# Last keys of two attention tiles: one 128x128 transpose, rounding and subtraction, then four DMAs, with late ends of value products

## The chip, the cores and the metric

The kernel runs on one core of a Trainium2 chip. The metric is device time in microseconds, and a change of more than about 0.2% either way is told apart from no change.

## What is computed

Attention on 8 batches of 8 heads, 576 positions and head width 64, in which only scores within `tau` of the row's maximum survive the softmax, and then a layer with weights `w_in` and `w_out` and the Mish function on all 4608 positions (`x` is the attention's output, positions by 512):

```
scores = scale * np.matmul(q, k.transpose(0, 1, 3, 2))
thresh = np.max(scores, axis=-1, keepdims=True) - tau
scores = np.where(scores >= thresh, scores, -1e9) - max
attn   = np.exp(scores) / (np.sum(np.exp(scores)) + 1e-09)
x      = np.matmul(attn, v)
h      = x @ w_in
out    = (h * np.tanh(softplus(h))) @ w_out
```

All is float32. The kernel gets that precision from TensorE by splitting an operand into a rounded part (`hi`, type fp32r) and the rest (`lo`), and multiplying both.

## The kernel before

Two stages follow each other. In the first, up to about 856 us of the span, attention and the product with `w_in` (`h`) run together; in the second the products with `w_out` run. The change touches the first stage only.

**Tiles.** A pair is two heads; its 2 x 576 query rows are 9 tiles of 128 rows, and there are 32 pairs, so 288 tiles, numbered `g`. The loop over `g` is written out by hand, and TensorE (PE), VectorE (DVE), ScalarE (ACT) and GpSimd (POOL) execute in the written order (class `InOrder`). The DMA queue of SyncE (SP) alone is ordered by a scheduler. In step `g` the loop issues the scores of tile g+1, the transposes of tile g-2, the evacuation of tile g-3, the value products of tile g-5 and some matmuls of `h`.

**A tile's way.** PE forms the scores `s` (two buffers). DVE takes the row maximum, ACT the exponential `e`, DVE masks and sums into `p`, POOL normalises `p`. PE transposes `p` (keys to partitions): four blocks of 128 keys into the PSUM tile `tp` (one buffer) and the last 64 keys, which are left over from 576 = 4 x 128 + 64, into `t5` (shown in the profile as `t`). ACT rounds to `hi`, DVE subtracts to `lo`. Pairs 0 to 3 (`FULL`) are treated in full precision and are not changed.

**The last keys.** For the other pairs, two tiles share one buffer `p`: an even tile `g-1` and the odd tile `g`. On the odd tile the last 64 keys of both are transposed in two transposes of 64 columns each, which land side by side on partitions 0 to 63 of `t5` (`transposes`). `tail_hi` (ACT) rounds these 64 x 256 values into partitions 0 to 63 of the ring `tk`, and `tail_lo` (DVE) writes the rest into partitions 64 to 127, so that one matmul per value product multiplies both. The ring holds 6 tiles of 128 columns.

**Value products.** `values` sums over the keys into a PSUM tile `y`: eight matmuls of the four blocks (`hi` and `lo`) and one or two matmuls on `tk` (`y<-tk`; two where the columns wrap in the ring). There are four products for each pair, after tiles 1, 4, 6 and 8 (`LAST`), 256 or 320 columns wide. `gather` copies the two halves of `y` to `x` and to a helper `yo` and adds them.

**Buffers in PSUM.** `t5`, `y` and `h` come from one pool of three buffers (`tag="ph"`); a new tile must wait until the last reader of the tile before it in that buffer is done: DVE's `tail_lo` for `t5`, ACT's copy to `hst` for `h`, ACT's copies of `gather` for `y`.

**How many `h` matmuls a step gets** stands in tables: `MIX_FIRST` for steps 42 to 77, `MIX` (period 18) for the next 180 steps, `MIX_LAST` for the last 36. Twelve matmuls make one `h` tile.

**SP's queue** carries the loads of `q`, `k` and `v` into the raw buffers (`r`, L316), the copies that join two heads for tile 4 of a pair (`kph`, `kpl`, `qph`, `qpl`, L382 and L384), the store of `h` (`hd<-hst`, L580) and of the last positions of `x` (`xd<-x`, L553). A load of `r` waits until POOL has read the buffer's old content.

Of the kernel before, what the change touches and what calls it, by code (L numbers as in the profile page):

```python
# [15 lines left out]
P = 128  # L16
B, H, S, D = 8, 8, 576, 64
# [5 lines left out]
XSPLIT = (4, 1, 1)  # L23
# [4 lines left out]
FULL = NP  # L28
# [37 lines left out]
    7: [(3, 0, 0, 128)],  # L66
    8: [(3, 128, 0, 128)],
}
MIX = (6, 6, 3, 4, 4, 7, 6, 7, 8, 3, 8, 2, 6, 2, 7, 3, 8, 6)
MIX_FIRST = (6, 6, 3, 4, 4, 7, 3, 7, 11, 3, 8, 2, 6, 2, 7, 5, 8, 6, 4, 6, 2, 5, 4, 7, 6, 7, 8, 3, 8, 2, 6, 2, 7, 3, 8, 6)  # L70
MIX_LAST = (6, 7, 8, 3, 8, 2, 6, 2, 8, 2, 8, 7, 5, 6, 3, 5, 4, 6, 6, 7, 8, 3, 8, 2, 6, 2, 8, 2, 8, 7, 5, 6, 3, 5, 4, 6)
DRAIN = 9
# [1 line left out]
LAST = {1: 0, 4: 1, 6: 2, 8: 3}  # L74
# [3 lines left out]
TK = 6 * P  # L78
# [5 lines left out]
def fv(ap):  # L84
    return ap.bitcast(F32)
# [104 lines left out]
def attention_moe(tc, q, k, v, tau, w_in, w_out, out):  # L190
# [3 lines left out]
    with ExitStack() as outer:  # L194
# [11 lines left out]
        with ExitStack() as first:  # L206
# [21 lines left out]
            with ExitStack() as att:  # L228
# [7 lines left out]
                pst = att.enter_context(tc.tile_pool(name="pst", bufs=1, space=PSUM))  # L236

                tkf, tk, fulls = ptp.tile([P, TK], F32, name="tkf", tag="tk", bufs=1), [], []
                both_e = sm.tile([P, 2, 2, HL + 2 * G], F32, name="e", bufs=1)
                smap, emap, turn = [], [], [0]  # L240
                for i in range(2):
# [133 lines left out]
                def join_heads(g):  # L375

                    made = pairs[g // 9]["ops"]
                    for a in range(2):
                        rows = slice(a * D, (a + 1) * D)
                        col = QCOL[4][a][1] + a * D  # L380
                        for to, k in zip(kpair, (made["k1"], made["k2"])):
                            nc.sync.dma_start(fv(to[rows]), fv(k[a][rows, D:]))  # L382
                        for i, to in enumerate(qpair):
                            nc.sync.dma_start(fv(to[rows, rows]), fv(made["qs"][a][i * D:(i + 1) * D, col:col + D]))  # L384

                def scores(g, t, first, qs, k1, k2, plain, **_):
                    s = smap[g % 2]
                    terms = []
                    if t == 4 and not plain:
                        first = 0  # L390
                        (kh, kl), (qh, ql) = kpair, qpair
                        terms = [(qh, kh), (ql, kh), (qh, kl)]
                    for a, col in () if terms else QCOL[t]:
                        cs = slice(col, col + P)
# [40 lines left out]
                def transposes(g):  # L435

                    both = tiles[g]["both"]
                    odd = g % 2
                    full = g < FULL * 9
                    at = odd * (S + D if full else S)  # L440
                    tp = pst.tile([P, 4, P], F32, name="tp")
                    for c in range(4):
                        nc.tensor.transpose(tp[:, c, :], both[:, at + c * P:at + (c + 1) * P], ident)
                    t5 = None
                    if full:
                        t5 = psh.tile([P, P], F32, name="t5", tag="ph")
                        end = 4 * P + (odd + 1) * D
                        nc.tensor.transpose(t5, both[:, end - P:end], ident)
                    elif odd:
                        t5 = psh.tile([P, 2, P], F32, name="t5", tag="ph")  # L450
                        for i in range(2):
                            nc.tensor.transpose(t5[:D, i], both[:, i * S + 4 * P:(i + 1) * S], ident)
                    return tp, t5

                def evacuate(t, tp, t5, pt):
# [24 lines left out]
                def tails(g):  # L480

                    if g % 2:
                        if not tk:
                            tk.append(ptp.tile([P, TK], F32R, name="tk", bufs=1))
                        at = (g - 1) * P % TK
                        cs = slice(at, at + 2 * P)
                        t5 = tiles[g]["tp"][1][:D].rearrange("p a b -> p (a b)")
                        yield tk[0][:D, cs], tk[0][D:, cs], t5

                def tail_hi(g):  # L490
                    for hi, lo, t5 in tails(g):
                        nc.scalar.copy(hi, t5)

                def tail_lo(g):
                    for hi, lo, t5 in tails(g):
                        nc.vector.tensor_tensor(lo, t5, fv(hi), ALU.subtract)

                def values_full(r, pt, vf, x):
                    main, tail = pt.pop(r)
# [14 lines left out]
                def values(pi, r, pt, vs, x, engine):  # L514
                    hi, lo = pt.pop(r)
                    n = WIDTH[r]
                    a = r // 2
                    y = psh.tile([P, 512], F32, name="y", tag="ph")
                    at = (pi * 9 * P + ROFF[r]) % TK
                    cut = min(n, TK - at)  # L520
                    ends = [(c, m, tk[0][:, (at + c) % TK:][:, :m]) for c, m in ((0, cut), (cut, n - cut)) if m]
                    main = [(0, n, p[:, c, :n]) for c in range(4) for p in (hi, lo)]
                    order = [(4, end) for end in ends]
                    order = [(0, main[0]), *order, *((i // 2, main[i]) for i in range(1, 8))]
                    for i, (c, (off, m, p)) in enumerate(order):
                        nc.tensor.matmul(
                            y[:, off:off + m], vs[:, a, c].rearrange("p a b -> p (a b)"), p,
                            start=i == 0, stop=i == len(order) - 1, skip_group_check=True,
                        )
                    mn = slice(a * D, a * D + D)  # L530
                    ot = slice((1 - a) * D, (1 - a) * D + D)
                    yo = sm.tile([P, 320], F32, name="yo", bufs=1)
                    xs = x[mn, XOFF[r]:XOFF[r] + n]

                    def gather():
                        nc.scalar.copy(xs, y[mn, :n])
                        nc.scalar.copy(yo[mn, :n], y[ot, :n])
                        engine.tensor_tensor(xs, xs, yo[mn, :n], ALU.add)

                    return gather  # L540
# [54 lines left out]
                chores = {}  # L595
                loads = {}
                adds = []
                pieces = []
                ready = []

# [6 lines left out]
                def begin(g):  # L607
                    pi, t = divmod(g, 9)
                    made = pairs[pi]["ops"]
                    tiles[g] = dict(s=scores(g, t, D if g % 2 == 0 or pi >= FULL else 0, **made))  # L610

                def product(g):
                    pi, t = divmod(g, 9)
                    pr = pairs[pi]
                    if t == 1:
                        pr["x"] = sm.tile([P, S], F32, name="x", bufs=2)
                    if t in LAST:
                        if pi < FULL:
                            some, gather = values_full(LAST[t], pr["pt"], pr["ops"]["vf"], pr["x"])
                            pieces.extend((work, None) for work in some[:-1])  # L620
                            pieces.append((some[-1], (gather, pi if t == 8 else None)))
                        else:
                            adds.append(values(pi, LAST[t], pr["pt"], pr["ops"]["vs"], pr["x"], nc.vector if g >= NT - 1 else nc.gpsimd))
# [21 lines left out]
                for g in range(NT + 5):  # L645
# [56 lines left out]
                        if closed is not None:  # L702
                            close_pair(g - XSPLIT[1], closed)
                    if g >= 12 + 9 * FULL and g % 9 == XSPLIT[0]:
                        close_pair(g, (g - XSPLIT[0]) // 9 - 1)
                    for work in chores.pop(g, []):
                        work()
                    for work in reversed(now):
# [40 lines left out]
                        warm_up(WARM[1 + g])  # L749
                    if not ahead and 2 <= g < NT + 2:  # L750
                        tiles[g - 2]["tp"] = transposes(g - 2)
                for step in sorted(chores):
                    for work in chores.pop(step):
                        work()
# [370 lines left out]
```

## Time and profile before

| | |
|---|---|
| median of three runs | 1299.0 us (1298.92 to 1299.88) |
| the profiled execution | 1298.43 us, its span 1296.6 us |
| granted TensorE clock, mean | 0.998 |
| busy: PE, DVE, ACT, POOL | 98%, 87%, 77%, 54% of the span |
| instructions | 27311 |

Busy shares are means over both stages. PE's matmuls overlap in the pipeline, and their ends are modelled, so the durations of single matmuls add up to more than the time that passed; the distance between starts, or the pieces of the chain of work that ended last, give what one costs. All operations of the engines are recorded by a helper on L98, so the profile is read by names of tiles.

### The profile page before, as it was taken

Reading aid. Unit: us, or ns where it says so; the run is one execution under the profiler, and the core shown is the slowest. Engines: PE = TensorE matmul, PEld = TensorE weight load, DVE = VectorE, ACT = ScalarE, POOL = GpSimd, SP = SyncE. Lnnn points to the kernel's source line nnn. Section 1 sums busy time; section 2 is a strip of 40 time slices with the busy share of each in tenths; the row PEclk is TensorE's granted clock in tenths of the full one; section 3 lists DMA queues with packets and bytes.
Section 4 is the critical chain, followed back from the end, with each engine's and each line's share of the span. In section 5 each row is a group of like instructions: output and inputs, shape, how many; then the busy total and the mean of one; then the engine's idle time right before and its main releaser. Section 6 shows DMA issues by size and latency. Waiting matters only on the chain.

```text
span 1296.6 us, 27311 instructions
## 1 busy us (share of the span) xinstructions
PE 1271.5 (98%) x8685; PEld 1154.4 (89%) x8685; DVE 1122.7 (87%) x3006; ACT 1000.0 (77%) x2060; POOL 695.8 (54%) x871
## 2 busy tenths in 40 slices
PE   8889999999999999999999999999999999999998
PEld 7667889988898898898998899878799999999998
DVE  7888999999999999999999999969868777878774
ACT  6889888888888888888888888776666676667663
POOL 5898877778778777787787777634000000000000
PEclk9999999999999999999999999999999999999999
DMA  6434544444444444454444444267544434443340
GB/s 218 148 112 114 147 121 137 129 121 147 130 124 144 118 141 129 117 148 133 124 135 124 144 128 117 76 204 244 187 146 131 155 131 147 164 153 110 119 125 33
DMA packets 151487, 177.43 MB, mean 137 GB/s; under 512 B 30000, under 2 KB 117040, under 8 KB 151344
## 3 DMA queue, kind: packets, MB, share of 16 engines
q1 hardware_dynamic: 148896, 171.37, 43.9%
q10 hardware_dynamic: 2448, 4.33, 0.9%
q8 instruction: 69, 1.13, 0.4%
q14 instruction: 74, 0.61, 0.1%
HBM read 109.05 MB, written 48.23 MB: 121 GB/s over the span
## 4 chain that ended last, share of the span: by engine, by line
PE 87%; DVE 6%; POOL 2%; ACT 2%; DMA 2%; issue 1%; SPq 0%; DVEq 0%; ACTq 0%; POOLq 0%
PE h L98 25%; PE y L98 19%; PE s L98 12%; PE x L98 10%; PE tp L98 9%; PE z L98 8%; PE t L98 2%; PE hx L98 2%; DVE un L98 2%; DVE p L98 1%; DVE st L98 1%; DVE dec L98 1%; DMA hd<-hst 1%; ACT e L98 0%; POOL dec L98 0%
## 5 line engine op out<-in xcount | busy, mean ns | idle before, releaser
L98 POOL TENSOR_SCALAR p<-p,st 128x576 f32<-128x576 f32 x288 | 240.5, 835 | 106.2 <-DVE st L98 95.9
L98 DVE SCALAR_TENSOR_TENSOR p<-s,st,e 128x580 f32<-128x580 f32 x288 | 236.4, 821 | 16.7 <-ACT e L98 6.0
L98 ACT ACTIVATE e<-s,st 128x580 f32<-128x580 f32 x288 | 215.6, 749 | 31.8 <-DVE st L98 23.9
L98 DVE TENSOR_REDUCE st<-s 128x1 f32<-128x580 f32 x288 | 218.2, 757 | 0.5
L98 PE MATMUL h<-xh,w1h 128*128 128x512 f32 x528 | 215.3, 408 | 0.0
L98 PE MATMUL h<-xl,w1h 128*128 128x512 f32 x528 | 211.9, 401 | 1.0 <-DVE xl L98 1.0
L98 PE MATMUL s<-k,q 128*128 128x290 f32 (+1 forms) x1056 | 195.6, 309 | 15.4 <-DVE p L98 15.2
L98 PE MATMUL h<-xh,w1l 128*128 128x512 f32 x528 | 209.7, 397 | 0.0
L98 PEld LDWEIGHTS s<-k,q 128*128 128x128 f32 x1056 | 168.9, 189 | 45.6 <-DVE p L98 26.5
L98 ACT CAST hi<-tp 128x512 fp32r<-128x512 f32 (+1 forms) x280 | 150.1, 547 | 74.8 <-PE tp L98 69.4
L98 DVE TENSOR_TENSOR ring<-un,ring 128x512 fp32r<-128x512 f32 x252 | 157.3, 690 | 54.4 <-ACT ring L98 54.3
L98 DVE TENSOR_TENSOR lo<-tp,hi 128x512 fp32r<-128x512 f32 (+1 forms) x280 | 173.7, 629 | 25.6 <-ACT hi L98 23.9
L98 PEld LDWEIGHTS tp<-ident,p 128*128 128x128 f32 x1152 | 142.0, 140 | 42.1 <-issue 4.7
L98 PE MATMUL tp<-ident,p 128*128 128x128 f32 x1152 | 173.3, 273 | 3.0 <-ACT pf L98 1.1
L98 ACT CAST ring<-un 128x512 fp32r<-128x512 f32 x252 | 138.9, 619 | 33.7 <-DVE un L98 33.0
L98 PE MATMUL y<-hi,vs 128*128 128x256 f32 (+1 forms) x448 | 135.3, 317 | 0.0
L98 PE MATMUL x<-ring,un 128*128 128x256 f32 x1152 | 134.7, 276 | 0.0
L98 PEld LDWEIGHTS x<-ring,un 128*128 128x128 f32 x1152 | 132.6, 188 | 0.0
L98 PE MATMUL y<-lo,vs 128*128 128x256 f32 (+1 forms) x448 | 123.1, 297 | 0.0
L98 POOL TENSOR_TENSOR x<-x,yo 64x256 f32<-64x256 f32 (+1 forms) x111 | 89.2, 804 | 55.4 <-ACT yo L98 54.4
L98 DVE TENSOR_TENSOR un<-un 128x1024 f32<-128x1024 f32 (+1 forms) x94 | 111.0, 1235 | 8.1 <-ACT un L98 8.1
L98 PEld LDWEIGHTS h<-xh,w1l 128*128 128x128 f32 x528 | 99.4, 188 | 13.4
(104 smaller groups left out, 2559.9 us busy)
## 6 DMA issues: line engine op xcount, KB each, us to landing
un<-hd SPq DMA_DIRECT2D x74, 512.0 KB, 4.7
hd<-hst SPq DMA_DIRECT2D x128, 256.0 KB, 2.6
r<-q SPq DMA_DIRECT2D x120, 160.0 KB, 2.8
r<-k SPq DMA_DIRECT2D x120, 160.0 KB, 2.3
r<-v SPq DMA_DIRECT2D x56, 160.0 KB, 2.4
kph<-k SPq DMA_DIRECT2D x56, 144.0 KB, 2.6
kpl<-k SPq DMA_DIRECT2D x56, 144.0 KB, 2.8
dec<-w_in SPq DMA_DIRECT2D x24, 256.0 KB, 2.9
```

Source lines behind the costliest of these rows:

```text
L98: made = method(*args, **kwargs)
```

## The change

1. The last keys of the odd tile are now read from the left end of its scores: `k` holds the last 64 keys ahead of all keys, and odd tiles of all pairs use keys in the order last 64, then 0 to 511 (`begin`, `join_heads`). With this the last keys of the even and of the odd tile lie next to each other in `p`, and one transpose of 128 columns brings them to `t5`: the even tile on partitions 0 to 63, the odd tile on 64 to 127.
2. ACT rounds 128x128 values into a new buffer `swap[:, 0]`, DVE subtracts into `swap[:, 1]`. Engines keep the partition here, and the ring needs `hi` on partitions 0 to 63 and `lo` on 64 to 127, so four DMAs of 64x128 values (32 KB each) on SP's queue carry `swap` into `tk`.
3. In `values` the matmuls on `tk` move from the second place to just before the last. A product of an even tile runs its first seven matmuls at the beginning of its step; the rest follows at the step's end, behind the step's transposes, and its `gather` in the next step. `close_pair` comes one step later for pairs whose last tile is even.
4. `yo` has no buffer of its own any more; it lies in the end of `r12`, which is unused then.
5. `MIX` is another distribution of the same 96 matmuls of `h` over 18 steps. `MIX_FIRST` and `MIX_LAST` stay.

```diff
-MIX = (6, 6, 3, 4, 4, 7, 6, 7, 8, 3, 8, 2, 6, 2, 7, 3, 8, 6)
+MIX = (6, 8, 2, 4, 2, 8, 6, 7, 10, 3, 8, 2, 4, 4, 5, 3, 8, 6)
...
+                swap = ptp.tile([P, 2, P], F32R, name="swap", bufs=1)
...
-                            nc.sync.dma_start(fv(to[rows]), fv(k[a][rows, D:]))
+                            nc.sync.dma_start(fv(to[rows]), fv(k[a][rows, first:first + S]))
...
-                        t5 = psh.tile([P, 2, P], F32, name="t5", tag="ph")
-                        for i in range(2):
-                            nc.tensor.transpose(t5[:D, i], both[:, i * S + 4 * P:(i + 1) * S], ident)
+                        t5 = psh.tile([P, P], F32, name="t5", tag="ph")
+                        nc.tensor.transpose(t5, both[:, 4 * P:5 * P], ident)
...
+                def tail_hi(g):
                     if g % 2:
+                        nc.scalar.copy(swap[:, 0], tiles[g]["tp"][1])
+
+                def tail_lo(g):
+                    if g % 2:
+                        nc.vector.tensor_tensor(swap[:, 1], tiles[g]["tp"][1], fv(swap[:, 0]), ALU.subtract)
                         if not tk:
                             tk.append(ptp.tile([P, TK], F32R, name="tk", bufs=1))
...
+                        for i in range(2):
+                            at = (g - 1 + i) * P % TK
+                            for j in range(2):
+                                to = tk[0][j * D:(j + 1) * D, at:at + P]
+                                nc.sync.dma_start(fv(to), fv(swap[i * D:(i + 1) * D, j]))
...
-                    order = [(0, main[0]), *order, *((i // 2, main[i]) for i in range(1, 8))]
...
+                    order = [*((i // 2, main[i]) for i in range(7)), *order, (3, main[7])]
+                    def run(n0, n1):
+                        for i, (c, (off, m, p)) in enumerate(order):
+                            if n0 <= i < n1:
...
-                    yo = sm.tile([P, 320], F32, name="yo", bufs=1)
+                    yo = r12.rearrange("p a b -> p (a b)")[:, -320:]
...
+                            if g % 2:
+                                run(0, 10)
+                                adds.append(gather)
+                            else:
+                                run(0, 7)
+                                finish.append((run, gather))
...
-                        close_pair(g, (g - XSPLIT[0]) // 9 - 1)
+                        pi = (g - XSPLIT[0]) // 9 - 1
+                        close_pair(g + (pi + 1) % 2, pi)
...
+                    while finish:
+                        run, gather = finish.pop(0)
+                        run(7, 10)
+                        adds.append(gather)
```

Three places show what that does to the order. The first is PE around the transposes of tile 157 and the product of the even tile 154, in the middle of the stage. Before (`t_7099` is the two transposes; the product of tile 154 had already ended):

```order
L98 MATMUL h<-xh,w1l 128x512
L98 MATMUL h<-xh,w1h 128x512
L98 MATMUL tp<-ident,p 128x128 x4
L98 MATMUL t_7099<-ident,p 64x128 x2
L98 MATMUL h<-xl,w1h 128x512
```

After, the same place:

```order
L98 MATMUL h<-xh,w1l 128x512
L98 MATMUL h<-xh,w1h 128x512
L98 MATMUL tp<-ident,p 128x128 x4
L98 MATMUL t_7219<-ident,p 128x128
L98 MATMUL y<-tk,vs 128x256
L98 MATMUL y<-lo,vs 128x256
L98 MATMUL h<-xl,w1h 128x512
```

One transpose stands where two stood, and behind it come the last two matmuls of the product of tile 154.

The second place is PE at tile 45, in the stretch of `MIX_FIRST`, with the numbers of the tiles. Before, behind the two transposes of `t5_2088`, the tile `h_2031` ends and the next one, `h_2121`, begins:

```order
L98 MATMUL tp_2083<-ident_76,p_1924 128x128 x4
L98 MATMUL t5_2088<-ident_76,p_1924 64x128 x2
L98 MATMUL h_2031<-xl_1755,w1h_92 128x512
L98 MATMUL h_2031<-xh_1754,w1l_93 128x512
L98 MATMUL h_2121<-xh_758,w1h_92 128x512
```

After, three matmuls of the product `y_2060` stand between (it wraps in the ring, so it has two on `tk`):

```order
L98 MATMUL tp_2087<-ident_76,p_1933 128x128 x4
L98 MATMUL t5_2092<-ident_76,p_1933 128x128
L98 MATMUL y_2060<-tk_1752,vs_1390 128x192
L98 MATMUL y_2060<-tk_1752,vs_1390 128x128
L98 MATMUL y_2060<-lo_1865,vs_1390 128x320
L98 MATMUL h_2042<-xl_1759,w1h_92 128x512
L98 MATMUL h_2042<-xh_1758,w1l_93 128x512
L98 MATMUL h_2134<-xh_759,w1h_92 128x512
```

In the built program `h_2121` lay in the buffer of an older `y`; `h_2134` lies in the buffer of `t5_2092`, which was written a few rows ahead, and its first matmul waits for a DVE instruction.

The third place is SP's queue in the middle of the stage. Before:

```order
L382 DMA kph<-k_3497 64x576
L382 DMA kpl<-k_3498 64x576
L580 DMA hd_68<-hst 128x512
L316 DMA r<-q 128x320 x2
L316 DMA r<-k 128x320 x2
L580 DMA hd_68<-hst 128x512
```

After:

```order
L494 DMA tk<-swap 64x128 x4
L384 DMA kph<-k_3541 64x576
L581 DMA hd_68<-hst 128x512
L384 DMA kpl<-k_3542 64x576
L317 DMA r<-q 128x320
L494 DMA tk<-swap 64x128 x2
L317 DMA r<-q 128x320
L494 DMA tk<-swap 64x128 x2
L317 DMA r<-k 128x320 x2
L581 DMA hd_68<-hst 128x512
```

The four copies to the ring stand between the loads; the first two of a group carry the rounded part and wait for ACT, the next two wait for DVE. Here the second two stand behind a load of `q`.

More of the change, by code (lines that the diff above doesn't have):

```diff
@@ L377, in join_heads @@
                     made = pairs[g // 9]["ops"]
+                    first = D if (g + 4) % 2 == 0 else 0
                     for a in range(2):
@@ L439, in transposes @@
                     full = g < FULL * 9
-                    at = odd * (S + D if full else S)
+                    at = odd * (S + D)
                     tp = pst.tile([P, 4, P], F32, name="tp")
@@ L478, in lo_main @@
                         nc.vector.tensor_tensor(lo[:, :, dst], tp[:, :, src:src + n], fv(hi[:, :, dst]), ALU.subtract)
-                def tails(g):
+                def tail_hi(g):
                     if g % 2:
+                        nc.scalar.copy(swap[:, 0], tiles[g]["tp"][1])
+                def tail_lo(g):
+                    if g % 2:
+                        nc.vector.tensor_tensor(swap[:, 1], tiles[g]["tp"][1], fv(swap[:, 0]), ALU.subtract)
                         if not tk:
                             tk.append(ptp.tile([P, TK], F32R, name="tk", bufs=1))
[L485 to L496, printed above, removed]
+                        for i in range(2):
[3 more added lines that the diff above has]
+                                nc.sync.dma_start(fv(to), fv(swap[i * D:(i + 1) * D, j]))
                 def values_full(r, pt, vf, x):
@@ L523, in values @@
                     order = [(4, end) for end in ends]
-                    order = [(0, main[0]), *order, *((i // 2, main[i]) for i in range(1, 8))]
[L525 to L529, printed above, removed]
+                    order = [*((i // 2, main[i]) for i in range(7)), *order, (3, main[7])]
+                    def run(n0, n1):
+                        for i, (c, (off, m, p)) in enumerate(order):
+                            if n0 <= i < n1:
+                                nc.tensor.matmul(
+                                    y[:, off:off + m], vs[:, a, c].rearrange("p a b -> p (a b)"), p,
+                                    start=i == 0, stop=i == len(order) - 1, skip_group_check=True,
+                                )
                     mn = slice(a * D, a * D + D)
                     ot = slice((1 - a) * D, (1 - a) * D + D)
-                    yo = sm.tile([P, 320], F32, name="yo", bufs=1)
+                    yo = r12.rearrange("p a b -> p (a b)")[:, -320:]
                     xs = x[mn, XOFF[r]:XOFF[r] + n]
@@ L538, in gather @@
                         engine.tensor_tensor(xs, xs, yo[mn, :n], ALU.add)
-                    return gather
+                    return run, gather
                 def operands_x():
@@ L597, in attention_moe @@
                 adds = []
+                finish = []
                 pieces = []
@@ L609, in begin @@
                     made = pairs[pi]["ops"]
-                    tiles[g] = dict(s=scores(g, t, D if g % 2 == 0 or pi >= FULL else 0, **made))
+                    tiles[g] = dict(s=scores(g, t, D if g % 2 == 0 else 0, **made))
                 def product(g):
@@ L622, in product @@
                         else:
-                            adds.append(values(pi, LAST[t], pr["pt"], pr["ops"]["vs"], pr["x"], nc.vector if g >= NT - 1 else nc.gpsimd))
+                            engine = nc.vector if g >= NT - 1 else nc.gpsimd
+                            run, gather = values(pi, LAST[t], pr["pt"], pr["ops"]["vs"], pr["x"], engine)
+                            if g % 2:
[4 more added lines that the diff above has]
+                                finish.append((run, gather))
                 def close_pair(g, pi):
```

## The prediction

> **What bounds the kernel.** I read the stretches of the span first, then the chain of work that ended last, then the groups. In the stretches the columns after the length are busy us (and instructions) of PE, PE's weight loads, DVE, ACT and POOL, then the granted clock and the DMA engines' share:
>
> ```profile
> 130.00:140.00 10.00, 7.57 (x40) 6.55 (x41) 9.85 (x28) 7.13 (x19) 9.59 (x13) 0.83 0.52 146
> 140.00:150.00 10.00, 9.94 (x60) 8.56 (x59) 9.50 (x30) 8.14 (x18) 7.92 (x10) 1.00 0.49 143
> 400.00:500.00 100.00, 100.00 (x650) 90.05 (x649) 95.16 (x298) 84.85 (x182) 78.33 (x96) 1.00 0.44 128
> 820.00:840.00 20.00, 20.00 (x134) 18.19 (x133) 19.08 (x60) 14.42 (x29) 9.66 (x12) 1.00 0.13 45
> PE s L98 <- DVE p L98: 15.2, 22, 1.2
> ```
>
> From about 140 to 856 us PE has no gap, and DVE is 95% busy behind it. The last row is PE's largest wait in all: 15.2 us in 22 waits. The chain says whether a "busy" PE really sets the pace. Its shares from 141 to 856 us, and then its pieces around tiles 154 to 156 (start, length, matmuls):
>
> ```profile
> by line: PE h L98 43.2%; PE s L98 19.1%; PE y L98 18.7%; PE tp L98 15.1%; PE t L98 3.8%; POOL x L98 0.1%; issue 0.0%; POOLq L98 0.0%
> 470.71 0.44 PE tp L98 x4
> 471.15 0.22 PE t L98 x2
> 471.37 0.70 PE h L98 x3
> 472.07 0.53 PE s L98 x4
> 472.60 0.93 PE h L98 x4
> 473.53 0.44 PE tp L98 x4
> 473.97 1.06 PE y L98 x9
> ...
> 378.39 1.40 PE y L98 x10
> ```
>
> The chain runs through PE alone, matmul after matmul. So in this stage a matmul less is time less, and every new wait of PE is time more. One transpose costs 0.11 us, a matmul of `h` 0.23, a 256-wide one of `y` 0.12, the four of `s` 0.53. The last row is a 320-wide product with two parts on the ring, together as wide as one: 1.40 / 9 = 0.156 for each 320 columns. The `t` transposes are 3.8% of 715 us = 27 us; half of them go.
>
> **The change part by part.** The rows of the last keys, with those that bound their new shapes:
>
> ```profile
> L98 PE MATMUL t<-ident,p 128*64 128x128 f32 x252 | 48.4, 274 | 0.0
> L98 DVE TENSOR_TENSOR tk<-t,tk 64x256 fp32r<-64x256 f32 x126 | 52.7, 418 | 3.9
> L98 DVE TENSOR_TENSOR lo<-tp,hi 128x512 fp32r<-128x512 f32 x224 | 152.8, 682 | 17.9 <-ACT hi L98 16.2
> L98 DVE TENSOR_TENSOR lo<-tp,hi 128x256 fp32r<-128x256 f32 x56 | 20.9, 416 | 7.7 <-ACT hi L98 7.7
> L98 ACT COPY hst<-h 128x512 f32<-128x512 f32 x132 | 77.5, 587 | 27.2 <-PE h L98 21.3 <-DMA hd<-hst 2.7 <-ACT dec L98 1.6
> ```
>
> (1) The transpose. 252 become 126. The chain belongs to PE from tile 41 on, so 124 odd tiles count: 124 x 0.11 = 13.6 us off the path. The new one has 128 weight columns instead of 64; its price I take as that of a `tp` transpose, 0.44 / 4 = 0.11, the same. The Trainium skill, "TensorE: Matmul & The Clock Gate", section "Back-to-back issue gap", gives about 81 ns as the sustained distance of matmuls with 128 columns. By that the gain would be an estimated 10.0 us and the sum below 1294.8; the chain's 0.11 us is float32 in this kernel, and the measurement decides.
>
> (2) DVE's subtraction. 64x256 takes 418 ns and 128x256 takes 416, so partitions do not count and columns do: 266 ns for 256 columns. 128x128 is then 416 - 133 = 283 ns, 0.135 us less. ACT's rounding shrinks alike. Neither is on the path; both only bring the data earlier. I count nothing.
>
> (3) The four DMAs, and when they must land. These rows show tile 155, DVE over one pair of tiles, and tile 45:
>
> ```profile
> 470.98 0.38 PE L98 MATMUL t<-ident,p 128*64 128x128 f32 x2
> 471.67 0.36 ACT L98 CAST tk<-t 64x256 fp32r<-64x256 f32 x1
> 472.70 0.42 DVE L98 TENSOR_TENSOR tk<-t,tk 64x256 fp32r<-64x256 f32 x1
> ...
> 467.63 0.82 DVE L98 SCALAR_TENSOR_TENSOR p<-s,st,e 128x580 f32<-128x580 f32 x1
> 473.15 0.82 DVE L98 SCALAR_TENSOR_TENSOR p<-s,st,e 128x580 f32<-128x580 f32 x1
> ...
> 153.76 0.38 PE L98 MATMUL t<-ident,p 128*64 128x128 f32 x2
> 155.32 0.42 DVE L98 TENSOR_TENSOR tk<-t,tk 64x256 fp32r<-64x256 f32 x1
> ```
>
> And the transfers (KB, median us to landing), the issue time of one of 64 partitions, and SP's longest kind of wait:
>
> ```profile
> un<-hd SPq DMA_DIRECT2D x74, 512.0 KB, 4.7
> hd<-hst SPq DMA_DIRECT2D x128, 256.0 KB, 2.6
> r<-q SPq DMA_DIRECT2D x120, 160.0 KB, 2.8
> r<-k SPq DMA_DIRECT2D x120, 160.0 KB, 2.3
> kph<-k SPq DMA_DIRECT2D x56, 144.0 KB, 2.6
> xd<-x SPq DMA_DIRECT2D x32, 32.0 KB, 2.2
> L382 SPq DMA_DIRECT2D kph<-k x56: 461/467/468, 107.3 to 816.9; - x56
> DMA to landing us min/median/max: 2.3/2.6/5.3
> SPq L316 <- POOL q L98: 205.2, 111, 4.5
> ```
>
> No row shows a copy from SBUF to the ring. Its landing lies between the 2.2 us of `xd<-x` (32 KB, the same size) and the 5.3 of the slowest `kph<-k`; I take 2.2, the nearest in size, and 0.47 us for the issue of each. For tile 155 ACT ends at 472.03, so the two rounded parts are issued by 473.0; DVE ends at 473.12 - 0.14 = 472.98, the even tile's rest is issued at about 473.1 and lands at 475.3. The even product of tile 154 is the tightest I find. In the new order 2 + 7 matmuls of `y`, 8 of `h`, 8 of `s` and 9 transposes stand between the start of that tile's transpose and `y<-tk`: 1.06 + 1.86 + 1.06 + 0.99 = 5.0 us, at 476.0. That leaves 0.7 us. An odd product (all four needed, its `y<-tk` eighth) has about 5.9 us after its transpose: landing at 475.8 is 4.8, margin 1.1. So I put the usual wait at zero and 0.5 us in all for stragglers; were all at 5.3 us, see the rivals. The old place of `y<-tk`, second in the product, had no such room. SP itself gets 504 issues of 0.47 us, 1.9 us for every 5.7 us of two tiles, in a queue that already waits (last row); a group can stand behind a load that waits for POOL, as the third quoted place of the order shows, up to 4.5 us. Loads of `r` come later too, by up to 1.9 us; ACT, 85% busy, takes that.
>
> (4) The late ends keep `y`'s buffer a step longer, and there are three buffers. Where `MIX_FIRST` and `MIX_LAST` rule, the second quoted place of the order comes twice in each: tiles 45, 63, 261, 279. The new `h` needs the buffer of a `t5` transposed just before. From the rows of tile 45: transpose at 153.76, DVE done at 155.74, 1.98 us, minus 0.14 = 1.84. PE arrives after one transpose (0.11), `y` of 192, 128 and 320 columns (0.31) and two `h` (0.47): 0.89. PE waits 0.95 us, four times 3.8 us. In `MIX` no `h` begins that close: counted in the same way, the narrowest places in its order leave 1.8 us for a `t5`, just what it takes here, and 1.1 us for a copy of `h` of 0.59 (last row of the fence above); zero. Bounds: nothing (if an earlier wait absorbs it) and, with tile 155's 2.14 us instead of 1.98, 4 x 1.1.
>
> (5) DVE's pace. From mask to mask two tiles take DVE 473.15 - 467.63 = 5.52 us without a gap; after, 5.38. PE's work from the transpose of tile 155 to that of 157 falls to 5.0, and `tp` has one buffer: PE must wait for DVE's subtraction there. Over 18 tiles DVE needs 9 x 5.38 = 48.4 us, PE about 50.9, so it is local: I take 0.15 us per 18 tiles, 14 such stretches, 2.1 us; bounds 0 and the whole 0.38, 5.3 us.
>
> (6) `yo` in `r12`, the other order of keys, `close_pair` and the new `MIX` have the same instructions as before; POOL's sums move by one step, and POOL is 78% busy there. Nothing, with the later closing covered because the last pair of a batch is odd and not delayed.
>
> **Sum.** -13.6 + 3.8 + 2.1 + 0.5 = -7.2 us. The profiled execution took 1298.43 us (0.6 below the median of the runs); 1298.4 - 7.2 = 1291.2 us. With the waits at their lower bounds it is 1284.8.
>
> **Rivals.**
> (A) The gain comes whole, 1284.8 us: the waits fall where PE would have waited anyway, or DVE's earlier end covers them. For it: PE waits nowhere today. Against it: the wait at tile 45 follows from two rows.
> (B) DVE becomes the pace-maker. The four tiles 153 to 157 hold the transposes closest; at the whole 0.38 us in (5) the sum is -13.6 + 3.8 + 5.3 + 0.5 = -4.0, 1294.4; with a second such place per 18 tiles it is 1298 and nothing is left. For it: DVE's 95%. Against it: DVE loses 0.135 us per two tiles where PE loses 0.11.
> (C) The ring is late, and the kernel is slower. A wait per even product begins when the rest lands 0.7 us later than I put it, at 2.9 us. With the four even products in 18 tiles 0.3 to 0.4 us apart in room (about 5.0, 5.4, 5.8 and 6.2 us after the transpose), landing at 4.0 us costs 1.1 + 0.7 + 0.3 = 2.1 us per 18 tiles, 14 times 29 us: 1320. It outweighs the gain of 7.2 from about 3.35 us on (0.5 us per 18 tiles). For it: twice the issues on SP, and its wait of up to 4.5 us for POOL. Against it: medians of 2.3 to 2.8 us for four to five times the bytes.
> (D) The four copies land one after the other, each 2.2 us after the last: the third lands at 472.1 + 6.6 = 478.7, 2.7 us late, and over four products 8.4 us per 18 tiles: about 1410. The rows speak against it: 74 x 4.7 + 128 x 2.6 + 120 x 2.8 + 120 x 2.3 + 56 x 2.6 = 1439 us of flights in a span of 1296.6, so flights overlap. The Trainium skill, "DMA: Bandwidth & Descriptors", section "Rules for kernel authors", says that two transfers to disjoint halves of the partitions serialize and that one of 128 partitions should be used; that is this rival, if it held for latency and not only for bandwidth.
>
> **Chances.** My forecast (some of the gain eaten in PSUM and on DVE, 1287 to 1295.5) 0.56, A 0.16, B 0.12, C 0.14, D 0.02. Within 0.2% is 1296.4 to 1301.6, about what a measurement tells from no change. Faster: 0.56 + 0.16 + half of B = 0.78, and I take 0.76, since waits may add up; same 0.10; slower 0.14. The range reaches from A, 1284.5, to the edge of B and the beginning of C, 1299.5.
>
> **What would show it.** Right: `t` with 126 matmuls, the `tk` subtraction at about 283 ns, PE still without gaps from 400 to 500 us, four waits of PE's `h` for DVE near 0.9 us at tiles 45, 63, 261 and 279. Wrong: PE waiting for DMA at `y<-tk` (C), for DVE's `lo` at `tp` more than 0.2 us per 18 tiles (B), or ACT waiting for `r`. The prediction fails if SP's queue falls behind, which no row of before can show.

## The result, and the profile after

The changed kernel takes 1316.1 us (median of four runs, 1315.8 to 1317.0), beside 1299.1 for the kernel before on the same chip: ratio 1.0131, interval 1.0113 to 1.0148. It is slower by 17 us, where 1291.2 was forecast and 1299.5 was the upper end. The profiled span is 1315.2 us.

The stretch from 400 to 500 us, in which PE had no gap before (columns as in the prediction):

```profile
400.00:500.00 100.00, 97.24 (x609) 85.33 (x609) 87.16 (x287) 79.21 (x178) 77.63 (x95) 1.00 0.53 154
```

PE, DVE and ACT are idler, DVE most (95.16 before). So PE no longer sets the pace alone, and DVE does not set it either. The shares of the chain that ended last, by line, name a new member:

```profile
PE h L98 24%; PE y L98 16%; PE x L98 10%; PE s L98 10%; PE z L98 7%; PE tp L98 7%; PE hx L98 4%; DMA tk<-swap 4%; DVE st L98 2%; ACT e L98 2%; DVE p L98 1%; PE t L98 1%; ACT hi L98 1%; POOL k L98 1%; SPq L494 1%
```

The copies to the ring are 4% of 1315 us, and SP's issue of them (L494) 1%. The waits (who, for whom: us in total, times, longest; PEld is PE's weight loads) say where this reaches PE:

```profile
PE y L98 <- DMA tk<-swap: 15.9, 23, 1.5
PEld h L98 <- DVE swap L98: 6.9, 11, 1.1
PE h L98 <- DVE swap L98: 2.6, 4, 0.7
```

PE's matmuls stand idle for the ring 15.9 us in `y<-tk`, and 2.6 us with `h` for the buffer of a `t5`. (The 6.9 us of the loads contain these four waits once more and are not added.) Shorter gaps count too: below, a delay is the distance between the starts of two neighbouring matmuls less the usual distance of such a pair, summed over 141 to 870 us. In this measure `y<-tk` is delayed by 23.0 us. The operations themselves have the sizes of the forecast; these are the groups from 141 to 870 us, with tile shapes:

```profile
L98 DVE TENSOR_TENSOR swap<-t,swap 128x128 fp32r<-128x128 f32 x123 | 34.6, 281 | 1.1 <-DMA tk<-swap 1.1
L98 ACT CAST swap<-t 128x128 fp32r<-128x128 f32 x123 | 33.7, 274 | 2.8 <-DMA tk<-swap 2.6
L98 PE MATMUL t<-ident,p 128*128 128x128 f32 x123 | 33.7, 274 | 0.0
```

The flights are no longer than forecast either (issue time and landing of line L494):

```profile
L494 SPq DMA_DIRECT2D tk<-swap x504: 461/552/1751, 129.5 to 873.8; - x168
...
DMA to landing us min/median/max: 1.7/1.9/4.5
```

A copy lands 1.9 us after the start of its issue, sooner than the 2.2 us assumed. What is late is the issue. Here is SP's queue up to 491 us (start, length):

```profile
485.03 0.38 SPq L554 DMA_DIRECT2D xd<-x  x1
485.53 0.37 SPq L317 DMA_DIRECT2D r<-q  x1
485.94 0.47 SPq L386 DMA_DIRECT2D qpl<-q  x1
486.46 0.59 SPq L386 DMA_DIRECT2D qph<-q  x1
487.39 0.46 SPq L386 DMA_DIRECT2D qpl<-q  x1
487.96 3.14 SPq L494 DMA_DIRECT2D tk<-swap  x4
491.20 0.55 SPq L384 DMA_DIRECT2D kph<-k  x1
```

DVE's subtraction for the four copies, and PE's product that reads them:

```profile
486.17 0.28 DVE L98 TENSOR_TENSOR swap<-t,swap 128x128 fp32r<-128x128 f32 x1
```

```profile
491.69 0.22 PE L98 MATMUL y<-tk,vs 128*128 128x128 f32 x1
492.54 0.33 PE L98 MATMUL y<-tk,vs 128*128 128x192 f32 x1 [0.63 <-DMA tk<-swap]
```

DVE has both parts ready at 486.45. SP comes to the copies at 487.96 and needs 3.14 us for four, back to back; the issue of the last begins at 490.52, and it lands 1.89 us later, at 492.4. PE stands at the ninth matmul of the product (the second on the ring) for 0.63 us. The chain of waits has the same piece:

```profile
489.92 0.55 SPq L494
490.52 1.89 DMA tk<-swap
492.54 0.49 PE y L98 x2
```

For comparison, SP's queue before, at about the same place in the program:

```profile
471.24 0.47 SPq L382 DMA_DIRECT2D kph<-k  x1
472.49 0.33 SPq L553 DMA_DIRECT2D xd<-x  x1
472.86 0.47 SPq L382 DMA_DIRECT2D kpl<-k  x1
473.38 0.59 SPq L384 DMA_DIRECT2D qph<-q  x1
474.27 1.31 SPq L316 DMA_DIRECT2D r<-q  x1
```

It had gaps. Over 300 to 800 us SP issued 441 DMAs before, 38% of the time; after it is 769 of 0.53 us each, 82%, and the median gap between two is 0.09 us. That is 82 issues for 18 tiles, 82 x 0.62 = 51 us, as much as PE's own work in 18 tiles (50.9 in the prediction). The queue has next to no slack left. The issue of the even tile's rest (third copy) begins 2.0 us after DVE's end (median of the groups of tiles 79 to 257), not 0.1, and it lands 4.0 us after DVE's end.

### The profile page after: what moved, and what is told of

It is laid out like the page before. It is cut to its first block, busy times and chain, and to the rows that moved or that the text cites. A ratio compares the mean times of both kernels' runs of the same rounds, so it can differ in the third digit from the quotient of the medians.

```text
span 1315.2 us, 28340 instructions
## 1 busy us (share of the span) xinstructions
PE 1270.1 (97%) x8559; PEld 1141.6 (87%) x8559; DVE 1091.3 (83%) x3006; ACT 981.6 (75%) x2060; POOL 694.4 (53%) x871
## 4 chain that ended last, share of the span: by engine, by line
PE 79%; DVE 5%; ACT 4%; DMA 4%; issue 3%; POOL 3%; SPq 1%; DVEq 0%; POOLq 0%; ACTq 0%
PE h L98 24%; PE y L98 16%; PE x L98 10%; PE s L98 10%; PE z L98 7%; PE tp L98 7%; PE hx L98 4%; DMA tk<-swap 4%; DVE st L98 2%; ACT e L98 2%; DVE p L98 1%; PE t L98 1%; ACT hi L98 1%; POOL k L98 1%; SPq L494 1%
## 5 line engine op out<-in xcount | busy, mean ns | idle before, releaser
L98 DVE TENSOR_REDUCE st<-s 128x1 f32<-128x580 f32 x288 | 218.1, 757 | 13.6 <-PE s L98 12.9
L98 PE MATMUL y<-hi,vs 128*128 128x256 f32 (+1 forms) x448 | 130.9, 315 | 0.0
L98 POOL TENSOR_TENSOR x<-x,un 64x256 f32<-64x256 f32 (+1 forms) x111 | 89.5, 806 | 76.4 <-ACT un L98 68.7
L98 PE MATMUL y<-lo,vs 128*128 128x256 f32 (+1 forms) x448 | 126.0, 297 | 0.0
L98 PEld LDWEIGHTS h<-xh,w1h 128*128 128x128 f32 x528 | 99.7, 189 | 16.6 <-DVE swap L98 6.9
```

The lines of the kernel that those rows point to most:

```text
L98: made = method(*args, **kwargs)
```

## The experiments

| kernel | us, median | ratio to before, interval |
|---|---|---|
| the change | 1316.1 | 1.0131 (1.0113 to 1.0148) |
| `reorder`: order alone | 1309.7 | 1.0074 (1.0059 to 1.0089) |
| `reorder_old_mix`: order alone, old `MIX` | 1315.6 | 1.0126 (1.0109 to 1.0143) |
| `no_copies`: the change without the four DMAs | 1296.5 | 0.9973 (0.9961 to 0.9984) |
| `two_copies`: two of the four | 1310.8 | 1.0079 (1.0064 to 1.0094) |
| `idle_copies`: before and four unread DMAs | 1303.4 | 1.0031 (1.0021 to 1.0040) |
| `light_sp`: the change, 16 of SP's 82 issues less | 1298.9 | 0.9999 (0.9990 to 1.0008) |
| `mix_all`: the change, `MIX` everywhere | 1314.7 | 1.0118 (1.0104 to 1.0132) |
| `light_mix`: both | 1296.8 | 0.9983 (0.9974 to 0.9992) |
| `direct_old`: one transpose, no `swap`, old order | 1300.5 | 1.0010 (1.0000 to 1.0019) |
| `direct_late`: the same in the new order | 1316.2 | 1.0130 (1.0115 to 1.0145) |
| `h_on_act`: the change, stores of `h` on ACT's queue | 1334.8 | 1.0272 (1.0252 to 1.0292) |
| `pool_moves`: POOL in the place of the DMAs | 1329.0 | 1.0229 (1.0215 to 1.0243) |

**`reorder`.** The kernel before with the late ends, the new `MIX` and `yo` in `r12`; two transposes and direct writes into the ring stay.

```diff
-                    order = [(0, main[0]), *order, *((i // 2, main[i]) for i in range(1, 8))]
+                    order = [*((i // 2, main[i]) for i in range(7)), *order, (3, main[7])]
...
+                                run(0, 7)
+                                finish.append((run, gather))
```

> The kernel before with the changed order alone (late ends of value products, the new MIX, yo in r12); two transposes and direct writes to the ring as before, no copies on SP. Theory 1, SP's queue is full (in the changed kernel 769 issues between 300 and 800 us, 0.53 us each, are 82% of the time, and about 0.1 us of waiting on the queue's own semaphores goes with each: 99%): the order costs only the PSUM buffer at four places, about 4 us, so 1299 to 1304. Theory 2, the copies are late by their own latency, not by the queue: the same, 1299 to 1304. Theory 3, the new order of PE itself loses the time (buffers of PSUM, single tp buffer): 1312 or more, and PE waits as long as in the changed kernel, but not for DMA.

The order alone costs 10.6 us, between the two ranges of the expectation. The lag behind the kernel before (difference of the starts of the same tile's transposes in the two traces) jumps by 1.2 to 1.3 us at tiles 45, 63, 261 and 279, and grows by 0.63 us for every 18 tiles between, under `MIX`, from 3.2 us at tile 78 to 9.5 at tile 258. PE at tile 45 shows the jump (in brackets the idle time before, and for whom):

```profile
153.55 0.38 PE L98 MATMUL t<-ident,p 128*64 128x128 f32 x2
...
154.37 0.40 PE L98 MATMUL h<-xh,w1l 128*128 128x512 f32 x1
155.70 0.47 PE L98 MATMUL h<-xh,w1h 128*128 128x512 f32 x1 [0.93 <-DVE tk L98]
```

The new `h` starts 1.33 us after the matmul ahead of it instead of 0.23. The growth between comes from the same wait: the trace has it at one tile of each 18 (number 83, 101, 119 and so on), about 0.5 us each time.

`reorder` has the long subtraction of before (418 ns). In the changed kernel the same place at tile 45 reads, on PE and on DVE:

```profile
154.51 0.27 PE L98 MATMUL t<-ident,p 128*128 128x128 f32 x1
...
155.23 0.40 PE L98 MATMUL h<-xh,w1l 128*128 128x512 f32 x1
156.27 0.50 PE L98 MATMUL h<-xh,w1h 128*128 128x512 f32 x1 [0.65 <-DVE swap L98]
...
155.94 0.28 DVE L98 TENSOR_TENSOR swap<-t,swap 128x128 fp32r<-128x128 f32 x1
```

The `h` stands idle for 0.65 us there and starts 1.04 us after the matmul ahead of it, a delay of 0.81.

**`reorder_old_mix`.** The same with the table of before.

```diff
-MIX = (6, 8, 2, 4, 2, 8, 6, 7, 10, 3, 8, 2, 4, 4, 5, 3, 8, 6)
+MIX = (6, 6, 3, 4, 4, 7, 6, 7, 8, 3, 8, 2, 6, 2, 7, 3, 8, 6)
```

> The kernel before with late ends, but with its old MIX: only that table differs from the run with the order alone. Theory, the order's loss is the new h that must wait for the buffer of a t5 written just ahead: in the traces that place costs 1.3 us at tiles 45, 63, 261 and 279, where the old tables rule, and 0.7 us per 18 tiles where the new MIX rules. With the old MIX it is there once in all 18 tiles: 14 x 1.3 = 18 us, 1315 to 1320. Rival, the late ends themselves cost (a y held a step longer, later sums): the table makes no difference, 1308 to 1312.

1315.6 us. In the groups the kind of matmul with which an `h` tile begins waits 13.1 us for DVE's `tk`, nearly twice the 7.2 of the same group in `reorder`:

```profile
L98 PE MATMUL h<-xh,w1h 128*128 128x512 f32 x528 | 214.0, 405 | 13.1 <-DVE tk L98 13.1
```

The lag grows by 1.23 us for 18 tiles under `MIX` instead of 0.63. Nothing else differs, so the growth is where `h` tiles begin, next to a `t5` that has just been written. The new table halves it and does not end it.

**`no_copies`.** The change without the four DMAs; the ring holds zeros, so the part of the last 64 keys is missing from the result.

```diff
+                            nc.vector.memset(fv(tk[0]), 0.0)
...
-                                nc.sync.dma_start(fv(to), fv(swap[i * D:(i + 1) * D, j]))
```

> The changed kernel without the four copies: the ring is set to zero once, so the last 64 keys of the rows from pair 4 on are missing in the output; the engines' work is the same. Theory 1 and 2: with the copies gone the gain of the transpose appears, -13.6 us and some +4 to +6 of waits for PSUM and DVE: 1289 to 1294. Theory 3: the loss stays, over 1305.

1296.5 us, above the 1289 to 1294 expected: 13.3 less than `reorder` (one transpose, smaller operations and the other order of keys), 19.7 less than the change (the copies). PE is nearly without gaps from 400 to 500 us:

```profile
400.00:500.00 100.00, 99.81 (x636) 88.18 (x635) 90.84 (x302) 82.13 (x184) 78.41 (x97) 1.00 0.45 131
```

From the kernel before over `reorder` and `no_copies` to the change these are three steps, 10.6 - 13.3 + 19.7 = 17.0 us. Such steps add up whatever the kernels do; that each would cost the same without the others is not shown by it, and `direct_late` below speaks against it.

**`two_copies`.** Only the rest (`lo`) is copied; its rounded part is missing from the result.

```diff
-                            for j in range(2):
+                            for j in (1,):
```

> The changed kernel with only the two copies of the unrounded rest (those that wait for DVE, the later ones); the rounded part of the last 64 keys from pair 4 on is missing in the output. SP issues 64 instead of 82 per 18 tiles. Theory 1: 64 x 0.64 = 41 us of 51, the queue keeps up, few waits at y<-tk, 1290 to 1296. Theory 2: the critical copy is still there, with the same latency behind DVE, so the waits at y<-tk stay: 1308 or more.

1310.8 us: half the copies take 14.3 of the 19.7 us, although SP's share of issue time from 300 to 800 us is only 59%. Of 13.8 us of delay at `y<-tk`, 11.9 stand at one product of each 18 tiles, that of tile 154 and of every 18th tile beside it, which the prediction found the tightest. For tile 190 SP, DVE and PE show why:

```profile
581.40 1.74 SPq L384 DMA_DIRECT2D kph<-k  x1
583.23 0.55 SPq L384 DMA_DIRECT2D kpl<-k  x1
583.83 0.59 SPq L386 DMA_DIRECT2D qph<-q  x1
584.47 0.59 SPq L386 DMA_DIRECT2D qpl<-q  x1
585.11 0.59 SPq L386 DMA_DIRECT2D qph<-q  x1
585.80 1.19 SPq L495 DMA_DIRECT2D tk<-swap  x2
...
582.08 0.28 DVE L98 TENSOR_TENSOR swap<-t,swap 128x128 fp32r<-128x128 f32 x1
...
587.79 0.35 PE L98 MATMUL y<-tk,vs 128*128 128x256 f32 x1 [1.72 <-DMA tk<-swap]
```

The data are ready at 582.36, and the copies stand behind five joins (the copies that join two heads) until 585.80. The first join is here one of the long issues (1.74 us); at tiles where it is not, the delay of this product is mostly about 0.7 us. So the cost is not in proportion to the number of copies, and it does not need a full queue: what stands directly ahead of the copies counts. In the change the same product has 11.4 of the 23.0 us; the other half is spread over other products, where `two_copies` has 1.9.

**`idle_copies`.** The kernel before, and four DMAs for each odd tile from the ring to a place that nobody reads.

```diff
+                        idle = r12.rearrange("p a b -> p (a b)")[:, -TK:]
...
+                                nc.sync.dma_start(idle[part, at:at + P], fv(tk[0][part, at:at + P]))
```

> The kernel before, with four copies of the same size per odd tile out of the ring into unused space; nothing reads them. Theory 1: SP needs 82 x 0.64 = 52.5 us per 18 tiles against 52.0 of PE, so the loads of q, k, v and the stores of h run late and the kernel gets slower though nobody waits for the copies: 1302 to 1320. Theory 2: nobody waits for them, 1299 to 1300.

1303.4 us. SP issues as much as in the change (85% of 300 to 800 us), and that costs 4.3 us. So a full queue is cheap here where no product waits for the copies.

**`light_sp`.** The joins are made for the first changed pair only, so tile 4 of the later pairs multiplies old values and its result is wrong. This takes load from SP and leaves the copies as they are.

```diff
-                    if g % 9 == 0 and FULL <= g // 9 < NPAIRS:
+                    if g == 9 * FULL:
                         join_heads(g)
```

> The changed kernel with the copies that join two heads for tile 4 (kph, kpl, qph, qpl) made for the first of the changed pairs only; tile 4 of the later pairs multiplies these old values. That takes 16 of about 82 issues per 18 tiles from SP's queue and nothing from any engine. Theory (the ring is late because SP issues without a pause): SP's share falls from about 99% to about 82%, the even tile's rest is issued about 1 us after DVE's end instead of 2.0, PE's waits for the ring fall from 23 us to 6 to 14, and the time is 1300 to 1309 us. Rival 1 (not the load but the place of the copies behind a burst of stores and loads): the waits stay near 14 to 20 us, 1309 to 1314. Rival 2 (the flight of the copies itself is too long for the place): 1315 to 1317, as the changed kernel.

1298.9 us, 17.2 less than the change, with all four copies in place and the same order on PE. SP's share is 63%. The median flight is 1.9 us as in the change; the issue of the even tile's rest now begins 0.5 us after DVE's end instead of 2.0. PE's waits for the ring:

```profile
PE y L98 <- DMA tk<-swap: 2.2, 4, 0.9
```

2.2 us instead of 15.9; the delay at `y<-tk` is 5.2 us instead of 23.0, and the difference, 17.8, is about the gain. SP's queue has gaps again:

```profile
470.01 0.33 SPq L317 DMA_DIRECT2D r<-k  x1
470.96 0.33 SPq L317 DMA_DIRECT2D r<-v  x1
471.80 0.33 SPq L317 DMA_DIRECT2D r<-q  x1
472.22 2.38 SPq L494 DMA_DIRECT2D tk<-swap  x4
474.79 0.44 SPq L581 DMA_DIRECT2D hd<-hst  x1
```

The second rival, the flight, does not hold, nor does the first in the words of the expectation: the stores and loads ahead of the copies are still there. But the run takes away the joins themselves, so it cannot tell their share of the load from their place ahead of the copies. `two_copies` bears on that: with the joins in place it has a lower share (59%) and a far greater cost, and the product of tile 154 and its like, delayed by 11.9 us there, is delayed by 1.0 here. So for that product, half of the change's delay, the place of the joins decides. For the other half the load is the likely cause, as it goes with half the copies as well as with the joins; no run leaves the load and moves the joins. 1298.9 is also a little below the 1300 that the theory gave.

**`mix_all` and `light_mix`.** The new `MIX` in the place of `MIX_FIRST` and `MIX_LAST`, first in the change, then in `light_sp`.

```diff
-                        n = DRAIN if g >= NT else MIX_FIRST[(step + 6) % 36] if b == 1 else MIX[g % 18] if b < B - 1 else MIX_LAST[step]
+                        n = DRAIN if g >= NT else MIX[g % 18]
```

> The changed kernel with the new MIX in the place of MIX_FIRST and MIX_LAST too (both begin at the same place of the 18 steps). Theory (a new h tile stands right behind t5 at tiles 45, 63, 261 and 279 and costs about 1.3 us each time, because the two old tables were not fitted to the late ends): the four steps of the lag go, 1310 to 1312.5 us. Rival 1 (the steps of the lag come from the late ends whatever the table): 1315 to 1317. Rival 2 (the first and last 36 steps need their own tables because h starts and ends there): over 1318.

> Both edits together: the joins made for the first changed pair only, and the new MIX in the place of MIX_FIRST and MIX_LAST. With SP's queue full, the table alone brought 1.4 us, although PE's waits for the buffer of t5 fell. Theory (SP then sets the pace of these 72 steps too, so that what PE saves there is lost again at the ring; with SP at about 63% issue time the saving shows): 3 to 5 us below the kernel with the joins left out alone, 1294 to 1296 us. Rival (the waits behind t5 in the old tables cost the end nothing, or the new table costs as much in other places): 1298 to 1300 us.

`mix_all` brought 1.4 us where 4 to 6 were expected. The four waits of PE's `h` behind `t5` (2.6 us) are gone, and those of the loads fell from 6.9 us to 3.6, but the waits for the ring did not fall (`mix_all`):

```profile
PE y L98 <- DMA tk<-swap: 16.2, 25, 1.5
...
PEld h L98 <- DVE swap L98: 3.6, 9, 0.5
```

As delays, `h` won about 3.3 us, and `tp` and the ring lost about 1.8 and 0.8. With the queue relieved (`light_mix` against `light_sp`, both with old values in tile 4) the same table brings 2.2 us, between the two expectations. The four long waits (0.7 us) of `PE h` are gone from the list, 2.5 us in all, and the loads of `h` wait 5.6 us instead of 8.2. The two numbers, 1.4 and 2.2, lie too close together to show that SP swallowed the table's gain. What the new table costs elsewhere in the first and last 36 steps was not separated.

**`direct_old` and `direct_late`.** No `swap` and no copies: ACT and DVE write into the ring in two operations of 64x128 each, for the even and the odd tile, behind the one transpose; first in the order of before, then in the new one.

```diff
+                        for i in range(2):
+                            at = (g - 1 + i) * P % TK
+                            rows = slice(i * D, (i + 1) * D)
+                            other = slice((1 - i) * D, (2 - i) * D)
+                            yield tk[0][rows, at:at + P], tk[0][other, at:at + P], tiles[g]["tp"][1][rows]
```

> One transpose of 128x128, but no copies and the order of before (ends second in the product, MIX of before): ACT rounds the two 64x128 halves of t5 in two operations straight into the ring, where each half stays on its partitions, and DVE writes the two rests in two operations to the other half of the partitions. Theory after the first runs (three separate terms: transpose about -13, order about +10.6, copies about +19.7): only the first remains, less what the second operation costs on DVE (2 x 283 - 418 = 148 ns per odd tile, DVE then needs 9 x 5.67 = 51.0 us per 18 tiles, PE 51.0): 1287 to 1293. Rival, DVE takes over as the pace-maker as soon as PE loses work: 1297 to 1302.

> The same direct writes, no copies, with the order of the changed kernel (late ends, new MIX, yo in r12). Three separate terms: 1296.5 as without copies, up to +4 for the second operations: 1296 to 1301. If the order's loss of 10.6 us belonged only to the two transposes: 1287 to 1293.

`direct_old` is the same as before (1300.5), as its rival had it, not the 1287 to 1293 of the theory. Here DVE writes each rest from one half of the partitions to the other, as its `tail_lo` did in the kernel before. So "Engines keep the partition here" is true of the change's operations over all 128 partitions only, and the DMAs are not the only way into the ring. The stretch and the groups show DVE as pace-maker:

```profile
400.00:500.00 100.00, 99.11 (x629) 87.20 (x628) 96.40 (x317) 86.91 (x200) 78.24 (x96) 1.00 0.44 129
```

```profile
L98 PE MATMUL tp<-ident,p 128*128 128x128 f32 x988 | 149.6, 274 | 6.2 <-DVE lo L98 6.1
L98 DVE TENSOR_TENSOR tk<-t,tk 64x128 fp32r<-64x128 f32 x248 | 71.5, 288 | 6.1
```

Two operations of 288 ns stand for one of 418, 0.16 us more in two tiles. PE now waits at `tp`; the delays there are 13.4 us (0.3 before), just what the transposes gave. `direct_late` missed by more: 1316.2 instead of 1296 to 1301, 19.7 above `no_copies`. Measured in the same way, 12.8 us stand at `tp` (3.7 in `no_copies`) and 15.9 at the first matmul of an `h` (6.3), since DVE frees `t5` later. That these two rise by 18.7 of the 19.7 us is read from the trace; which of ACT's and DVE's second operations is to blame was not tried.

**`h_on_act`.** The change with the stores `hd<-hst` on ACT's DMA queue instead of SP's.

```diff
-queue = nc.sync if len(chunks) == 1 or n >= 16 else nc.scalar
+queue = nc.sync if len(chunks) > 1 and n >= 16 else nc.scalar
```

> The changed kernel with the stores of h issued from ACT's queue instead of SP's: 73 instead of 82 issues per 18 tiles on SP, and ACT gets 9 x 0.33 us. Theory, the copies stand late in SP's queue: 3 to 9 us come back, 1307 to 1313. Rival, the copies are late by their own landing: 1315 to 1318.

1334.8 us, 18.7 more than the change instead of less. ACT issues in its own order, and the next rounding waits for that:

```profile
489.67 0.34 ACTq L98 DMA_DIRECT2D hd<-hst  x1
490.05 0.59 ACT L98 CAST hi<-tp 128x512 fp32r<-128x512 f32 x1 [0.41 <-ACT hst L98]
```

SP's share of issue time fell from 82% to 73%, and the delays at `y<-tk` only from 23.0 to 18.6 us, while those at `tp` rose from 2.6 to 20.7: PE waits for ACT's `hi` and then DVE's `lo`, which hold `tp`.

**`pool_moves`.** The order of before, one 128x128 transpose, rounding and subtraction, the ring read eighth; POOL copies `swap` into the ring.

```diff
-                                nc.sync.dma_start(fv(to), fv(swap[i * D:(i + 1) * D, j]))
+                                nc.gpsimd.tensor_copy(to, fv(swap[i * D:(i + 1) * D, j]))
```

> One transpose, rounding and subtraction of 128x128 as in the changed kernel, but the order and the MIX of before without late ends; the products read the ring eighth instead of second, and the four moves from swap into the ring are copies of 64x128 on POOL instead of DMAs. Theory (the costs of the change are SP's queue and the order, and DVE with 283 ns instead of 418 keeps up): the transposes' 13 us are won and the moves hide in POOL's slack (four of about 0.25 us per two tiles, 78% busy before, about 95% after): 1286 to 1292 us. Rival (POOL has no room for it: its 80 us of waits for DVE are needed, p comes late and PE waits at tp): 1300 to 1325 us.

1329.0 us, slower even than its rival's 1300 to 1325. POOL's busy share of 400 to 500 us (fifth engine) goes from 78.33 to 93.58%, and PE's weight loads wait for it:

```profile
400.00:500.00 100.00, 95.69 (x603) 84.14 (x601) 87.06 (x286) 79.22 (x177) 93.58 (x158) 1.00 0.43 123
```

```profile
PEld y L98 <- POOL tk L98: 30.0, 34, 1.3
```

No kernel here that computes everything is faster than the one before.

## Why the prediction was wrong

**(1) The transpose: right.** -13.6 us were forecast. In the trace of the kernel before the starts of the two transposes of a tile lie 0.109 us apart (mean of 124), 13.5 us in all. `no_copies` against `reorder` gives -13.3, but that holds more than the transpose: the delays at `h` shrink by about 3.4 us and those at `tp` grow by about 1.5 as well. So the chain's price of 0.11 holds and the 81 ns of the Trainium skill, "TensorE: Matmul & The Clock Gate", section "Back-to-back issue gap", does not for these float32 transposes.

**(2) The smaller operations: right.** 281 ns for DVE (283 forecast), 274 for ACT.

**(3) The four DMAs: the step that failed.** It forecast 0.5 us, and the copies cost 19.7. The landing was not the error: 1.9 us, below the 2.2 assumed. The error is the sentence "the even tile's rest is issued at about 473.1", 0.1 us after DVE's end; the median is 2.0 us. The step counted SP's new work, 1.9 us for every 5.7, but never added what SP already had: 441 issues in 500 us, 46 for 18 tiles, became 82, and with 0.53 us each (not 0.47) and 0.09 us between two that fills the 50.9 us of PE's work. A margin of 0.7 us cannot stand that. `light_sp` shows that it is SP's queue: with 16 issues less, and not one of them a copy, the kernel comes within 2.4 us of `no_copies`. But a sum of issues alone would not have told the cost either: `two_copies`, with SP at 59%, still loses 14.3 us, since the joins stand directly ahead of the copies of the very product that step (3) called the tightest.

**(4) The buffer behind `t5`: mechanism right, size too small.** The four places are the four forecast. In the changed kernel the delay is 0.81 us at each (0.95 forecast), 3.2 us in all for 3.8. The 0.93 us of `reorder` lie nearer to 0.95, but by luck: that kernel has the longer subtraction, for which the step had taken off 0.14 us. The sentence "In `MIX` no `h` begins that close ... zero" failed. In `no_copies`, where no late copy covers it, the ten places under `MIX` are delayed by about 0.26 us each, so that the term is about 5.9 us and not 3.8. With the long subtraction of `reorder` the growth is 0.63 us for 18 tiles, 6.3 us from tile 78 to tile 258, and the order costs 10.6. Leaving exactly as much room as the buffer takes is not zero cost; `reorder_old_mix` doubles it with another table.

**(5) DVE's pace: about right.** 2.1 us at `tp` were forecast; the delays there are 3.7 us in `no_copies` and 2.6 in the change. Rival B did not come: DVE's subtraction shrank by 0.137 us in two tiles, PE's transposes by 0.109. `direct_old`, in which DVE's work grows by 0.16 us instead, shows it at full size.

**(6) The rest: not separated.** `reorder` holds `yo`, `close_pair` and the new `MIX`, and its 10.6 us are about the four jumps (5 us) and the growth (6.3 us) together; what is left for these edits is below what the traces can tell. The other order of keys has no run of its own.

**The rivals.** C, the late ring, was what happened. Its cause, SP's queue, stands in step (3), in C and in the last sentence of the prediction, but without a size. It gave 29 us for a flight of 4.0 us, that is a landing 4.1 us after DVE's end; the third copy landed at 4.0 and the copies cost 19.7. Its beginning, a flight of 2.9 us, was too late: `light_sp` has a median landing 2.9 us after DVE's end and still 5.2 us of delay at `y<-tk`, since the late groups count and not the median. In B the second place gives 1299.7 by its own sum (-13.6 + 3.8 + 10.6 + 0.5 from 1298.4), not 1298; nothing else rests on it. D did not come: the issues of the copies begin 0.60 us apart (median), and a copy still lands 1.9 us after the start of its own, so their flights overlap. The rule of the Trainium skill, "DMA: Bandwidth & Descriptors", section "Rules for kernel authors", that transfers to disjoint halves of the partitions serialize, does not show in their latency at this spacing.

## What to carry to other kernels

When a change adds DMAs, add up the issues of their queue over one period, with the gaps between them, and compare that with the period of the engine that sets the pace; flight time says nothing of it. Then read what stands directly ahead of each copy that a product waits for. In these runs the share of issue time alone did not tell the cost: 85% without a reader cost 4.3 us, 59% with the joins ahead of the copies 14.3, and 63% without the joins 2.4. Such a copy must not stand behind a burst on its queue, or it must have a margin as long as the longest burst ahead of it. A wait of the busiest engine that another order would open is to be counted for each repeat, even where the room seems to be just enough.

## What the runs showed of the hardware

The issue of one DMA of 64 partitions is not a constant of 0.46 us. In the full queue its median is 0.55 us and its longest 1.75; in `light_sp` the median is 0.55 too, and the longest 2.10. Between 141 and 870 us 37 issues of the change and 32 of `light_sp` take over 0.75 us, stores, loads and copies alike, and many of them lie about 20 us apart. What makes them long was not settled.

The four 32 KB copies within SBUF land 1.9 us after the start of their issue (median), sooner than every load and store in the prediction's rows.

A copy of 64x128 on POOL takes 289 ns, about what DVE needs for a subtraction of that size (288) and more than ACT's rounding (261).
